# Rewriting an attention and gated feed-forward kernel around equal 512-column blocks, with loads on GpSimd's queue

## Chip, cores and metric

The kernel runs on one core of one Trainium2 chip. The metric is the device time of one execution in microseconds, lower being better. Kernels that are compared ran on the same chip in the same rounds, and only executions in the fast state are compared. Three runs of the kernel before were known, with a median of 392.63 us (390.9 to 392.78). The experiments ran on several chips, where the kernel before took 392.2 to 394.2 us (medians), so a few us between two experiments mean little.

The engines are named as the profile names them: PE is TensorE (matrix multiplications), DVE is VectorE, ACT is ScalarE, POOL is GpSimd, SP is SyncE. "Granted clock" is the share of its full clock that TensorE was allowed.

## The reference

```python
# q, k, v: (8 batches, 8 heads, 576 positions, 64), float32
def attention(q, k, v):
    theta = pi / 2 * arange(576) / 576
    phi = lambda x: concat([relu(x) * cos(theta), relu(x) * sin(theta)], -1)
    qp, kp = phi(q), phi(k)                     # 64 columns become 128
    kv = einsum('bhsf,bhsd->bhfd', kp, v)
    z = kp.sum(axis=2)
    return einsum('bhsf,bhfd->bhsd', qp, kv) / (einsum('bhsf,bhf->bhs', qp, z) + 1e-6)

x = attention(q, k, v)                          # as (4608 tokens, 512)
out = (gelu(x @ w_gate) * (x @ w_val)) @ w_out  # 512 -> 1536 -> 512
```

Each batch needs these steps: loads of q, k and v; *preps* (relu times cosine or sine, on VectorE); the *q turn*, which puts the features of the prepared q on the partitions; kv and then five numerators with their divisions; the *x turns*, which put the channels of x on the partitions; and then the three large multiplications. The large multiplications are nearly all of TensorE's work, so the rest has to be hidden behind them.

## The kernel before

All loads, the q turns and the stores go through one queue, SyncE's, in program order. The staging buffers come in threes.

```python
inp = ctx.enter_context(tc.tile_pool(name="inp", bufs=3))
xtp = ctx.enter_context(tc.tile_pool(name="xtp", bufs=3))
# ...
def load(name, src, b, half, pieces=1):
    t = inp.tile([128, 2, R * D], FP32, name=name)
    # ...
        nc.sync.dma_start(out=t[:, m:m + step], in_=view[:, 2 * half + m:2 * half + m + step])

def prep(name, b, pair, part, n=1):
    # ... for m in range(pair, pair + n):
        nc.vector.scalar_tensor_tensor(        # two sources: the input and the table
            dst[:, m, :, part * D:(part + 1) * D],
            src[:, m % 2].rearrange("p (j d) -> p j d", j=R),
            0.0,
            tab[:, :, None].to_broadcast([128, R, D]),
            op0=ALU.max, op1=ALU.mult)

def turn_q(b, pair0, n):
    # ... for i in range(2):
        nc.sync.dma_start_transpose(out=qT[b][i]..., in_=src[64 * i:64 * i + 64, ...])
```

The main loop has one 448-column block and seven of 512. In each of its twelve *slots* a block multiplies 128 columns of both weights ("gate" and "value"), and hides a piece of the next batch's attention:

```python
segs = [(576, 448)] + [(BLK * i, BLK) for i in range(2, 9)]
for si, (c0, n) in enumerate(segs, start=1):
    b = si + 1
    for jt in range(JT):
        gv_unit(c0, n, jt)
        if b < B:
            s = jt - (3 if si == 1 else 0)
            if s == 0: prep_pairs("qp", b, 0)
            if s == 1: prep_pairs("qp", b, 2)
            if s == 2: turn_q(b, 0, 4); prep_pairs("kp", b, 0)
            if s == 3: prep_pairs("kp", b, 2); cast_v(b, 0); cast_v(b, 1)
            if s == 5:
                if b + 1 < B: load_batch(b + 1)     # SyncE queue, behind the turn
                kv_unit(b)
            if 6 <= s < 6 + NT: nm_unit(b, s - 6)   # numerator and division
            if 7 <= s < 7 + NT: xt_unit(b, s - 7)   # x turned by TensorE
        if si >= 2: o_part(...)                     # output of the block before
    # ... (the first block does its last numerators after the loop)
```

## Time and profile before

| before | value |
|---|---|
| span of the profiled run | 392.7 us |
| TensorE busy | 342.5 us, 87% |
| mean granted clock | 0.950 |
| q turn, first issue to last landing | 10.5 to 12.3 us |
| loads of q, k, v, issue to landing (median) | 5.0, 7.2, 9.7 us |

These are lines of the profile's page of the kernel before: busy time by engine, three rows of the span in 40 slices (tenths), and the one queue that carries nearly everything (packets, MB, share of 16 DMA engines).

```profile
PE 342.5 (87%) x2484; PEld 177.1 (45%) x2484; DVE 204.6 (52%) x379; ACT 128.7 (33%) x242; POOL 36.8 (9%) x35
...
PE   2588955899576988998999999979997999999995
...
PEclk9999986599888998999999999989999999999999
DMA  8989908029495099309933990597056111111214
...
q1 hardware_dynamic: 57440, 55.45, 51.7%
```

TensorE is full in the later two thirds, and the losses lie early. The table by stages says where. Its columns are the stretch, its length, the busy time and instruction count of each engine, the granted clock, the DMA share and GB/s.

```profile
0.00:26.50 26.50, 13.20 (x169) 10.10 (x170) 18.10 (x30) 14.46 (x28) 11.67 (x15) 1.00 0.95 321
26.50:62.40 35.90, 29.61 (x194) 19.66 (x192) 20.32 (x46) 14.89 (x28) 11.13 (x8) 0.92 0.69 236
62.40:75.80 13.40, 7.40 (x133) 5.97 (x133) 8.31 (x21) 3.47 (x8) 0.00 (x0) 0.63 0.41 58
75.80:88.60 12.80, 12.80 (x53) 5.42 (x51) 0.00 (x0) 2.13 (x4) 0.00 (x0) 0.82 0.24 55
88.60:128.70 40.10, 29.34 (x237) 15.17 (x236) 24.22 (x43) 10.49 (x20) 4.77 (x4) 0.87 0.72 209
128.70:378.00 249.30, 239.80 (x1662) 116.27 (x1660) 133.19 (x239) 80.33 (x149) 9.21 (x8) 0.99 0.45 111
```

The start takes 26.5 us, the burst of batch 1's attention (third row) runs at a clock of 0.63, and in the last row TensorE is busy for 239.8 of 249.3 us. This is the ordering in the timeline of SyncE (start, length of the issue, what was issued):

```profile
247.79 3.47 SPq L220 DMA_TRANSPOSE qT_2743<-qp  x1
251.35 4.29 SPq L220 DMA_TRANSPOSE qT_2744<-qp  x1
255.73 2.23 SPq L359 DMA_DIRECT2D out_dram<-o_sb  x2
258.01 1.72 SPq L71 DMA_DIRECT2D qf<-in_q_dram  x2
```

The two halves of the turn are followed by a store, and only then by the loads for the batch after. The waits view has one line per turn, each of 0.8 to 2.6 us; this is the longest (engine, what waited, on what: total us, times, longest):

```profile
PE nm L260 <- DMA qT_2744<-qp: 2.6, 1, 2.6
```

### The profile page before, as it was taken

What the parts mean: (1) busy time and instruction counts of PE and PEld (TensorE: products, weight loads), DVE (VectorE), ACT (ScalarE), POOL (GpSimd) and SP (SyncE); (2) the same over time, 40 slices, a digit from 0 to 9 for tenths busy, and PEclk for the clock granted to TensorE, in tenths of its full rate; (3) what the DMA queues carried; (4) which work ended last, traced back from release to release, by engine and by line L of the source; (5) the groups of instructions that cost most, each with busy time, mean ns of one, the idle gap of its engine ahead of it and who ended that gap; (6) DMA issues with size and microseconds to landing.
All of it is one profiled execution on the core that took longest, in us unless ns stands there. A gap on an engine that the chain in (4) does not pass through costs nothing.

```text
span 392.7 us, 6081 instructions
## 1 busy us (share of the span) xinstructions
PE 342.5 (87%) x2484; PEld 177.1 (45%) x2484; DVE 204.6 (52%) x379; ACT 128.7 (33%) x242; POOL 36.8 (9%) x35
## 2 busy tenths in 40 slices
PE   2588955899576988998999999979997999999995
PEld 2365633544243444544544454535443544444442
DVE  6653496504945873587449556915693522222210
ACT  5755421213123331433333242314232333223321
POOL 1821530000202000200020011002000000000000
PEclk9999986599888998999999999989999999999999
DMA  8989908029495099309933990597056111111214
GB/s 265 381 278 362 388 15 120 2 66 357 65 222 214 2 142 321 128 1 126 340 126 44 192 350 6 86 246 258 2 84 118 29 27 42 40 27 28 52 42 95
DMA packets 57467, 55.83 MB, mean 142 GB/s; under 512 B 34912, under 2 KB 39008, under 8 KB 57440
## 3 DMA queue, kind: packets, MB, share of 16 engines
q1 hardware_dynamic: 57440, 55.45, 51.7%
q8 instruction: 19, 0.31, 0.3%
q14 instruction: 8, 0.07, 0.0%
HBM read 37.75 MB, written 9.44 MB: 120 GB/s over the span
## 4 chain that ended last, share of the span: by engine, by line
PE 71%; DMA 14%; DVE 8%; ACT 3%; POOL 2%; issue 1%; ACTq 0%; DVEq 0%; POOLq 0%
PE gv_ps L332 41%; PE o_ps L370 17%; PE gv_ps L370 6%; DVE qp L151 4%; PE xt L309 3%; PE nm L260 3%; DMA qT_1449<-qp 2%; DMA qT_3175<-qp 2%; DMA qT_2744<-qp 2%; DMA qT_1113<-qp 2%; DMA qT_702<-qp 2%; DMA qT_1881<-qp 2%; DVE hT L345 2%; DMA qT_2312<-qp 2%; DVE x_sb L273 1%; POOL pos L178 1%
## 5 line engine op out<-in xcount | busy, mean ns | idle before, releaser
L345 DVE TENSOR_TENSOR hT<-gel,gv_ps 128x512 bf16<-128x512 f32 (+2 forms) x132 | 76.0, 589 | 152.2 <-ACT gel L340 152.0
L340 ACT ACTIVATE gel<-gv_ps 128x512 f32<-128x512 f32 (+2 forms) x120 | 66.5, 555 | 203.9 <-PE gv_ps L332 203.0
L332 PE MATMUL gv_ps<-xT,wg_sb 128*128 128x512 bf16 x336 | 88.7, 388 | 0.0
L332 PE MATMUL gv_ps<-xT,wv_sb 128*128 128x512 bf16 x336 | 87.5, 383 | 0.0
L370 PE MATMUL o_ps<-wo_sb,hT 128*128 128x512 bf16 x336 | 87.1, 382 | 0.0
L332 PEld LDWEIGHTS <-wg_sb 128*128 128x128 bf16 x480 | 47.6, 101 | 64.0 <-issue 18.0
L332 PEld LDWEIGHTS <-wv_sb 128*128 128x128 bf16 x480 | 48.6, 101 | 49.9 <-issue 4.2
L370 PEld LDWEIGHTS <-hT 128*128 128x128 bf16 x432 | 41.2, 100 | 44.7 <-issue 3.5
L332 PE MATMUL gv_ps<-xT_335,wg_sb 128*128 128x288 bf16 (+1 forms) x144 | 30.0, 335 | 11.2 <-DVE hT L345 10.9
L332 PE MATMUL gv_ps<-xT_335,wv_sb 128*128 128x288 bf16 (+1 forms) x144 | 30.3, 339 | 0.0
L151 DVE SCALAR_TENSOR_TENSOR qp<-qf,cos_t 128x576 bf16<-128x576 f32 x32 | 26.0, 849 | 2.5 <-DMA qf<-in_q_dram 2.4
L151 DVE SCALAR_TENSOR_TENSOR kp<-kf,cos_t 128x576 bf16<-128x576 f32 x32 | 25.9, 851 | 1.5 <-DMA kf<-in_k_dram 1.5
L273 DVE TENSOR_TENSOR x_sb<-nm,rec 128x512 bf16<-128x512 f32 x34 | 23.5, 692 | 1.2
L370 PE MATMUL gv_ps<-wo_sb,hT 128*128 128x512 bf16 x96 | 23.3, 407 | 0.0
L151 DVE SCALAR_TENSOR_TENSOR kp<-kf,sin_t 128x576 bf16<-128x576 f32 x30 | 22.3, 788 | 0.0
L151 DVE SCALAR_TENSOR_TENSOR qp<-qf,sin_t 128x576 bf16<-128x576 f32 x30 | 21.4, 752 | 0.0
L309 PE MATMUL xt<-ident,x_sb 128*128 128x128 bf16 x144 | 15.6, 238 | 4.2 <-DVE x_sb L273 3.2
L187 POOL CAST vx_132<-vf 128x1152 bf16<-128x1152 f32 x7 | 8.7, 1250 | 112.1 <-DMA vf<-in_v_dram 77.9
L379 ACT COPY o_sb<-o_ps 128x512 f32<-128x512 f32 x28 | 16.4, 586 | 7.4 <-PE o_ps L370 7.4
L187 POOL CAST vx_134<-vf 128x1152 bf16<-128x1152 f32 x8 | 9.2, 1150 | 102.0 <-DMA vf<-in_v_dram 102.0
L317 ACT COPY xT<-xt 128x512 bf16<-128x512 bf16 (+1 forms) x34 | 16.7, 501 | 4.8 <-PE xt L309 4.7
L237 PEld LDWEIGHTS <-kp 64*128 64x128 bf16 x576 | 11.0, 100 | 9.7 <-issue 4.0
(77 smaller groups left out, 171.9 us busy)
## 6 DMA issues: line engine op xcount, KB each, us to landing
out_dram<-o_sb SPq DMA_DIRECT2D x72, 128.0 KB, 2.4
qf<-in_q_dram SPq DMA_DIRECT2D x14, 576.0 KB, 5.0
kf<-in_k_dram SPq DMA_DIRECT2D x14, 576.0 KB, 7.2
vf<-in_v_dram SPq DMA_DIRECT2D x14, 576.0 KB, 9.7
wgf<-in_moe_w_gate_dram SPq DMA_DIRECT2D x4, 768.0 KB, 6.6
wvf<-in_moe_w_val_dram SPq DMA_DIRECT2D x4, 768.0 KB, 7.8
wof<-in_moe_w_out_dram SPq DMA_DIRECT2D x4, 768.0 KB, 12.6
qf<-in_q_dram SPq DMA_DIRECT2D x4, 288.0 KB, 4.1
```

The lines of the kernel that those rows point to most:

```text
L151: nc.vector.scalar_tensor_tensor(dst[:, m, :, part * D:(part + 1) * D], src[:, m % 2].rearrange("p (j d) -> p j d", j=R), 0.0, tab[:, :, N ...
L187: copy(vx_tiles[b % 2][:, 2 * half:2 * half + 2, :, 0:D], staged["vf", b, half].rearrange("p m (j d) -> p m j d", j=R),)
L237: nc.tensor.matmul(ps[:, i, pair * (D + 1):(pair + 1) * (D + 1)], lhsT=kp[rr, pair, j, :], rhs=vx[rr, pair, j, :], start=(j == 0), stop=(j ...
L260: nc.tensor.matmul(ps[:, h // 4, (h % 4) * (D + 1):(h % 4 + 1) * (D + 1)], lhsT=qT[b][h % 2][:, h // 2, c0:c0 + 128], rhs=kv_sb[b][:, h // ...
L273: nc.vector.tensor_tensor(x, nm[:, :, :, 0:D], rec[:, :, :, None].to_broadcast([128, 2, 4, D]), op=ALU.mult,)
L309: nc.tensor.transpose(out=ps[:, ct, :], in_=x[:, ct * 128:(ct + 1) * 128], identity=ident)
L317: nc.scalar.copy(xt[:, :, base + c:base + c + m], ps[:, :, o:o + m])
L332: nc.tensor.matmul(ps[:, 0:n], lhsT=w[:, ct, js], rhs=xt[:, ct, cc:cc + n], start=(ct == 0), stop=(ct == CT - 1),)
L340: nc.scalar.activation(gel[:, 0:n], g_ps[:, 0:n], AF.Gelu)
L345: nc.vector.tensor_mul(hT[hb][:, jt, c:c + m], gel[:, o:o + m], v_ps[:, o:o + m])
L370: nc.tensor.matmul(o_ps[i], lhsT=hT[blk][:, jt, tt * 128:(tt + 1) * 128], rhs=wo_sb[:, jt, :], start=(jt == 0), stop=(jt == JT - 1),)
L379: nc.scalar.copy(o_sb, o_ps.pop(i))
```

## The change

The change is a rewrite that tries to keep TensorE full from earlier on. All blocks have 512 columns. Weights are converted by the DMA that loads them, so no engine casts them. The loads of weights and of batches 1 to 7 form one queue in a fixed order, issued by GpSimd. Preps use an instruction with one source and a scalar per partition. The eight accumulator banks are assigned by hand. Attention runs one block ahead. In batches 2 to 7, x is turned by DMA instead of TensorE.

```diff
-    wst = ctx.enter_context(tc.tile_pool(name="wst", bufs=4))
-    inp = ctx.enter_context(tc.tile_pool(name="inp", bufs=3))
+    inp = ctx.enter_context(tc.tile_pool(name="inp", bufs=2))      # now a whole batch each
+    xsp = ctx.enter_context(tc.tile_pool(name="xsp", bufs=3))
@@ weights, cut @@
-            nc.sync.dma_start(out=t[:, :, 0:n * 128], in_=src[:, :, sl])
+        nc.gpsimd.dma_start(out=wg_sb[:, :, sl], in_=wg_r[:, :, sl])
+        nc.gpsimd.dma_start(out=wv_sb[:, :, sl], in_=wv_r[:, :, sl])
@@ prep, cut @@
-            nc.vector.scalar_tensor_tensor(
+                nc.vector.tensor_scalar(
+                    o, i, 0.0, tab[:, j:j + 1], op0=ALU.max, op1=ALU.mult
+                )
@@ x, cut @@
+            nc.sync.dma_start_transpose(
+                out=xT_block(blk)[:, :, c:c + m], in_=x[o:o + m, :]
+            )
@@ the main loop, cut @@
+    for n in range(1, NB):
+        b = n + 1
         for jt in range(JT):
+            gv_unit(n, jt)
             if b < B:
+                if jt < 2:
+                    prep("q", b, jt, range(R))
+                if jt == 2:
+                    turn_q(b)
+                if jt in (2, 3):
+                    prep("k", b, jt - 2, range(R))
+                if jt == 4:
+                    kv_unit(b)
                     if b + 1 < B:
-                        load_batch(b + 1)
+                        for name in ("q", "k", "v"):
+                            for m in (0, 2):
+                                load(nc.gpsimd, name, b + 1, m, m + 2)
+                        for m in (0, 2):
+                            cast_v(b + 1, m, m + 2, pool_copy)
+                if 5 <= jt < 5 + NT:
+                    nm_unit(b, jt - 5)
+                    turn_x(b, jt - 5)
+            o_part(4 * (n - 1) + jt // 3, range(4 * (jt % 3), 4 * (jt % 3) + 4), 4 + (jt // 3) % 2, act_copy)
```

The place of the load in the program text (slot 4) says little. GpSimd has its own instruction stream and reaches the load long before TensorE reaches slot 4. What holds the load is its buffer. With two buffers, q of batch b+1 needs the buffer of batch b-1, and the program orders it behind the reads that must be finished. So what GpSimd loads beside the turn of batch b is batch b+2.

## The prediction

> **What bounds the kernel now.** TensorE. In the last stage the PE timeline repeats every 2.59 us (8 gate/value matmuls 1.73, 4 output matmuls 0.86): 0.216 us per 512-column matmul. The feed-forward's 1296 are 280 us of 392.6; 112.6 us are start, attention, waits and tail. Table of stages: first gate/value matmul at 26.5 us; block 0 until 62.4; q turn and attention burst until 75.8, clock 0.61; output projection until 88.6; the 448-column block until 128.7; seven blocks in 249.3 us (217.7 of feed-forward, 31.6 for five batches, 6.3 each); tail 14.7.
>
> Of a batch's 6.3 us PE work is 4.0 (kv 1.35, five numerators 1.4, five transposes 1.15). The chain of waits names the rest: preps, two pairs of 1.43 us between hT multiplies, stretch four slots from 2.59 to about 3.27; the q turn, 10.5 to 12.3 us from first issue to last landing, holds the first numerator 1 to 3 us.
>
> **What changes.**
> 1. Start: no staging casts; two token tiles suffice for the first half-width matmuls. Estimate from today's durations: v lands near 10 us, first gate/value matmul near 18.
> 2. Block 0: about 25 us of PE work and 3 of waits; its projection (10.4) hides batch 1's attention (4). Block 1 starts near 62 (now 88.6, though 64 columns, 2.6 us, further on).
> 3. Preps become one-source. The Trainium skill, "VectorE: DVE Perf Modes", section on the perf-mode tier table, gives fp32 SBUF single-source ops twice the rate. A traced prep takes 0.67 us back to back for 576 elements (1 per cycle plus 0.07). Estimate at double rate: 0.20 us per 256 elements, 1.8 us a slot instead of 2.7; with hT it fits 2.59.
> 4. x transposes leave PE in batches 2 to 7 (1.15 us each), but as many bytes as the q turn's join the DMA transposes.
> 5. Apparently unintended: output tiles 0 to 3 are computed after block 0 and again inside block 1: 48 matmuls, 10.4 us for nothing.
>
> **On the critical path.** 62 + 8 × 31.1 + 6 × 2.85 (kv, numerators) + 14.7 = 342.5 us, plus each batch's wait for its q turn. Preps end about 7 us into a block, so it lands near 18; the first numerator is due at 16: 2 us of wait. Traffic makes it worse: loads two batches ahead wait only for preps to free their buffers, so q's load is released just as the turn is issued, k and v soon after. "DMA: Bandwidth & Descriptors" (same skill), section "Issuing engines are not separate DMA queues", says they share 16 engines; before, one in-order queue put the turn first, and the turn alone shows a DMA share near 1.0 for 9 us; the loads take 9.6. Full sharing would cost up to 8 us per batch in blocks 1 to 4. I take 3 us for each of six batches, 18 us.
>
> **Prediction: 361 us**, 343 to 386 eight times in ten. Faster by over 2%: 0.87; within 2%: 0.09; slower: 0.04.
>
> **Right or wrong in the profile.** First gate/value matmul 16 to 21 us; block 1 begins 59 to 66; preps near 0.2 us; slots of 2.6 us at a block's start; each batch's first numerator the largest PE wait, on a DMA into qT, worse in blocks 1 to 4 than in 5 and 6; otherwise clock near 1.00; 480 output matmuls instead of 432.
>
> **What would make it wrong.** The q turn drowned by loads (then about 385, clock dropping after each wait), or winning the sharing (about 352). Preps at single rate (+1 us per slot). GpSimd's descriptors slow, so weights late and block 0 starved. x turns late for the next block.

## The result and the profile after

The rewrite gives correct outputs and takes 481.38 us (four runs, 478.76 to 482.74) where the kernel before took 391.79 us (four runs, 390.9 to 392.78). The ratio is 1.2258, 95% interval 1.2202 to 1.2313: 23% slower. Ratios here are the mean time of one kernel's fast runs over that of the other's of the same rounds, so they differ a little from the ratio of the quoted medians.

The page of the profile after:

```profile
PE 349.2 (73%) x2343; PEld 172.1 (36%) x2378; DVE 198.8 (42%) x550; ACT 105.1 (22%) x197; POOL 58.4 (12%) x82
...
PE   7599629920799405996039970599799799999996
...
PEclk9699869975699955999559995599999999999999
DMA  7999996699343995329972299642732822111113
...
q1 hardware_dynamic: 55616, 25.18, 38.2%
q0 software_dynamic: 14112, 30.15, 25.5%
```

TensorE's busy time has hardly moved (342.5 to 349.2 us), but the span is 84 us longer. There are four deep holes in the TensorE row, evenly spaced; the granted clock falls to half in each, and the DMA row is full beside them. The line of the chain of work that ended last names them, as shares of the 477.0 us:

```profile
DMA qT<-qp 30%; PE ps L310 28%; PE ps L336 16%; DVE qp L158 7%; DVE kp L158 5%; PE ps L243 3%; DVE hT L319 3%; DMA kf<-in_k_dram 1%; DVE x_sb L256 1%; PE ps L224 0%; PE ps L291 0%; PE ps L187 0%; PE ps L201 0%; DVE vx L163 0%; DVE rec L255 
```

The waits view gives the same in time lost by TensorE:

```profile
PE ps L243 <- DMA qT<-qp: 104.0, 12, 20.9
```

TensorE stood 104.0 us waiting for turned q, up to 20.9 us at once. Before, each turn had cost it 0.8 to 2.6 us.

To see when the holes arise I took the start of each block (its first write of the hidden tile by VectorE, less the 2.0 us that the first slot takes before it) and compared the lengths with the prediction's own terms. For blocks 1 to 6 that is 31.1 + 2.85 + 3 = 36.95 us.

| | block 1 starts | 1 | 2 | 3 | 4 | 5 | 6 | 7 | block 8 and tail |
|---|---|---|---|---|---|---|---|---|---|
| predicted | 62 | 36.95 | 36.95 | 36.95 | 36.95 | 36.95 | 36.95 | 31.1 | 45.8 |
| measured | 80.3 | 62.6 | 61.6 | 61.5 | 58.2 | 37.6 | 37.9 | 31.1 | 46.3 |

The sums for blocks 5 to 8 are right within a microsecond, for 5 and 6 partly by luck: the 3 us were meant for loads beside the turn, of which there are none, and block 5 spends instead 2.2 us waiting for the turn and about 1.5 in four slots that the preps hold at 2.97 us (see the end). Blocks 1 to 4 are too short by 96.0 us in the prediction and the start by 18.3; together these are all but 2 us of the 116 by which the profiled span (477.0) exceeds 361. What blocks 1 to 4 have and 5 and 6 don't is a load of a further batch: in block 5 batch 7, the last, has already been loaded.

The timelines of SyncE and of GpSimd in block 1 show what stands beside what. SyncE:

```profile
88.37 22.29 SPq L180 DMA_TRANSPOSE qT<-qp  x2
110.75 1.29 SPq L330 DMA_DIRECT2D out_dram<-o_sb  x2
```

GpSimd, with its idle time before each instruction and what ended it in brackets:

```profile
88.60 1.42 POOL L80 DMA_DIRECT2D qf<-in_q_dram  x2 [10.91 <-DVE qp L158]
94.71 1.42 POOL L80 DMA_DIRECT2D kf<-in_k_dram  x2 [4.68 <-DVE kp L158]
96.12 1.41 POOL L80 DMA_DIRECT2D vf<-in_v_dram  x2
```

The last q prep of batch 2 frees q's buffer and at the same time allows the turn. So the load of batch 4's q follows the turn's issue by 0.2 us, in this block and in the next two (151.20 after 150.96, 212.80 after 212.56). k and v follow six microseconds later, when the k preps end. The turn then lands at 122.5, 34.1 us after its issue; in blocks 2 to 4 it takes 33.3, 33.2 and 30.0 us. In blocks 5 and 6, with nothing beside, it takes 11.8 and 12.1. The loads suffer too: their medians are 12.8, 19.0 and 20.8 us instead of 5.0, 7.2 and 9.7.

The stretch in detail, in the table by windows (columns as above):

```profile
core 0: us, PE busy (x) PEld busy (x) DVE busy (x) ACT busy (x) POOL busy (x), PEclk, DMA share, GB/s
...
90.00:94.00 4.00, 3.71 (x26) 1.62 (x24) 4.00 (x15) 0.60 (x1) 0.02 (x1) 1.00 1.12 142
...
102.00:106.00 4.00, 0.00 (x0) 0.00 (x0) 0.00 (x0) 0.00 (x0) 0.00 (x0) 0.50 1.03 238
...
110.00:114.00 4.00, 0.00 (x0) 0.00 (x0) 0.00 (x0) 0.00 (x0) 0.00 (x0) 0.50 1.22 55
...
122.00:126.00 4.00, 3.43 (x15) 1.51 (x16) 1.06 (x3) 0.59 (x1) 1.15 (x1) 0.50 0.25 74
```

From 102 to 114 no compute engine works at all, the DMA engines count as fully busy, and yet from 110 to 114 they move 55 GB/s. A share near 1 tells here that packets were in flight, not that bytes flowed. The DMA view of three windows of 2 us shows it by queue (packets, MB, share of the 16 engines' time). In order they are 90 to 92 us (the turn has the engines, the load isn't yet moving), 104 to 106 us (both), and 112 to 114 us (both, in the last third):

```profile
q1 hardware_dynamic: 1046, 0.27, 102.1%
...
q0 software_dynamic: 122, 0.51, 74.2%
q1 hardware_dynamic: 165, 0.04, 41.6%
...
q1 hardware_dynamic: 135, 0.03, 90.2%
q0 software_dynamic: 15, 0.06, 21.7%
```

q1 is SyncE's queue and carries the turn, in packets of 256 bytes; q0 is GpSimd's. The turn alone gets 1046 packets through in 2 us; beside the loads it gets 165, and later 135. The time of one turn packet, as share × 32 us / packets, goes from 31 ns to 81 and then to 214 ns. The turn doesn't merely get a smaller share of a constant flow: in the last window both queues together move less than the turn alone would.

### The profile page after: what moved, and what is told of

It reads as the page before. It is cut to its first block, busy times and chain, and to the rows that moved or that the text cites. A ratio compares the mean times of both kernels' runs of the same rounds, so it can differ in the third digit from the quotient of the medians.

```text
span 477.0 us, 6176 instructions
## 1 busy us (share of the span) xinstructions
PE 349.2 (73%) x2343; PEld 172.1 (36%) x2378; DVE 198.8 (42%) x550; ACT 105.1 (22%) x197; POOL 58.4 (12%) x82
## 3 DMA queue, kind: packets, MB, share of 16 engines
q0 software_dynamic: 14112, 30.15, 25.5%
## 4 chain that ended last, share of the span: by engine, by line
PE 49%; DMA 31%; DVE 17%; issue 2%; SPq 0%; ACT 0%; DVEq 0%; ACTq 0%
DMA qT<-qp 30%; PE ps L310 28%; PE ps L336 16%; DVE qp L158 7%; DVE kp L158 5%; PE ps L243 3%; DVE hT L319 3%; DMA kf<-in_k_dram 1%; DVE x_sb L256 1%; PE ps L224 0%; PE ps L291 0%; PE ps L187 0%; PE ps L201 0%; DVE vx L163 0%; DVE rec L255 0%
## 5 line engine op out<-in xcount | busy, mean ns | idle before, releaser
L319 DVE TENSOR_TENSOR hT<-gel,ps 128x512 bf16<-128x512 f32 (+1 forms) x114 | 74.9, 657 | 140.7 <-PE ps L310 140.6
L336 PE MATMUL ps<-wo_sb,hT 128*128 128x512 bf16 x457 | 123.1, 393 | 2.1 <-issue 1.2
L310 PE MATMUL ps<-xT,wg_sb 128*128 128x512 bf16 (+1 forms) x452 | 115.8, 379 | 1.2 <-DVE xT L295 1.1
L310 PE MATMUL ps<-xT,wv_sb 128*128 128x512 bf16 (+1 forms) x448 | 115.0, 377 | 0.5
L318 ACT ACTIVATE gel<-ps 128x512 f32<-128x512 f32 (+1 forms) x114 | 65.5, 575 | 158.1 <-PE ps L310 150.5
L243 PE MATMUL ps<-kv_sb,qT 128*128 128x65 bf16 x320 | 19.6, 203 | 104.7 <-DMA qT<-qp 104.0
L336 PEld LDWEIGHTS <-hT 128*128 128x128 bf16 x480 | 45.1, 100 | 48.9 <-issue 3.8
L243 PEld LDWEIGHTS <-qT 128*128 128x128 bf16 x320 | 16.6, 104 | 116.4 <-DMA qT<-qp 107.8
L345 ACT COPY o_sb<-ps 128x512 f32<-128x512 f32 x38 | 22.3, 586 | 152.0 <-PE ps L336 150.0
L256 DVE TENSOR_TENSOR x_sb<-ps,rec 128x512 bf16<-128x512 f32 x40 | 27.7, 691 | 1.6 <-DVE rec L255 0.2
L80 POOL DMA_DIRECT2D qf<-in_q_dram x15 | 10.8, 720 | 96.0 <-DVE qp L158 93.8
L158 DVE TENSOR_SCALAR kp<-kf,cos_t 128x256 bf16<-128x256 f32 (+1 forms) x81 | 21.5, 338 | 1.4 <-DMA kf<-in_k_dram 1.4
L158 DVE TENSOR_SCALAR qp<-qf,cos_t 128x256 bf16<-128x256 f32 x72 | 19.9, 349 | 2.5 <-DMA qf<-in_q_dram 2.5
L158 DVE TENSOR_SCALAR qp<-qf,sin_t 128x256 bf16<-128x256 f32 x72 | 20.0, 349 | 0.0
L224 PEld LDWEIGHTS <-kp 64*128 64x128 bf16 x504 | 12.2, 99 | 14.6 <-DVE kp L158 9.2
## 6 DMA issues: line engine op xcount, KB each, us to landing
qf<-in_q_dram POOLq DMA_DIRECT2D x14, 576.0 KB, 12.8
vf<-in_v_dram POOLq DMA_DIRECT2D x14, 576.0 KB, 20.8
```

The costliest lines, as they stand in the source:

```text
L80: eng.dma_start(out=staged[name, b][:, m0:m1, j0 * D:j1 * D], in_=rows(srcs[name], b)[:, m0:m1, j0 * D:j1 * D],)
L158: nc.vector.tensor_scalar(o, i, 0.0, tab[:, j:j + 1], op0=ALU.max, op1=ALU.mult)
L224: nc.tensor.matmul(bank(6 + i)[:, m * (D + 1):(m + 1) * (D + 1)], lhsT=kp[rr, m, j, :], rhs=vx[rr, m, j, :], start=(j == 0), stop=(j == R ...
L243: nc.tensor.matmul(bank(b0 + h // 4)[:, (h % 4) * (D + 1):(h % 4 + 1) * (D + 1)], lhsT=qT[b][h % 2][:, h // 2, c0:c0 + 128], rhs=kv_sb[b][ ...
L256: nc.vector.tensor_tensor(x, nm[:, :, :, 0:D], rec[:, :, :, None].to_broadcast([128, 2, 4, D]), op=ALU.mult,)
L310: nc.tensor.matmul(bank(b0 + g)[:, 0:w], lhsT=wt[:, ct, js], rhs=xt[:, ct, c0:c0 + w], start=(ct == 0), stop=(ct == CT - 1),)
```

## The experiments

Thirteen kernels ran, all correct. Each is an edit of the rewrite. The letters in the expectations name the theories that they compare; each expectation spells them out. The main ones are: that the loads run beside the turn (A), that the excess over plain sharing belongs to GpSimd's software queue (B, later A2), and that the x turns by DMA are to blame (C). Times are medians, and ratios are to the kernel before in the same rounds, with 95% intervals. In e1, e2, e3, e5, e6 and e9 the place of the load in the program, or the gate before it, also lets it run only one batch ahead: beside (or after) the turn of batch b comes batch b+1, of the same size, where the rewrite has b+2.

### e1_gate: hold the loads until the turn has landed

GpSimd reads one column of both halves of the turned q before it issues the next loads. Queue and sizes stay.

```diff
+    def gate_on_turn(b):
+        for i in range(2):
+            nc.gpsimd.tensor_copy(gate, qT[b][i][:, 0, 0:1])
@@
                     if b + 1 < B:
+                        gate_on_turn(b)
                         for name in ("q", "k", "v"):
```

> Changed kernel, but GpSimd reads one column of both halves of the turned q before it issues the next batch's loads, so loads still go through GpSimd's queue but never run beside the q turn. Theory A (loads running beside the turn stretch both): the q turn takes 11 us again in every block instead of 34, the wait at the first numerator falls from 20-24 to 2-3 us in all blocks, time near 395 us (481 less 4 times about 21). Theory B (GpSimd's queue is itself slow, descriptors late): loads stay slow, 20 us and more to land, time above 440. Theory C (the turns of x make too much DMA work): no large change, above 450.

It took 390.69 us (0.9946, 0.9841 to 1.0051). All turns of blocks 1 to 5 took 11.8 to 12.4 us, and the wait for turned q fell from 104.0 to 16.6 us:

```profile
PE ps L243 <- DMA qT<-qp: 16.6, 7, 2.8
```

So the loads beside the turn are the cause of the stretch. The queue by itself isn't slow (theory B): after the turn its loads landed in 5.1, 9.3 and 12.6 us (medians). A part of the gain was lost elsewhere: the loads now fall on the x turns. The group of the division says so (busy, mean ns, idle before it, what ended that):

```profile
L256 DVE TENSOR_TENSOR x_sb<-ps,rec 128x512 bf16<-128x512 f32 x40 | 27.7, 691 | 30.9 <-DMA xT<-x_sb 29.6 <-DVE rec L255 0.2
```

VectorE waited 29.6 us for x turns to give a buffer back.

### e2_sp_queue: the loads in SyncE's queue, behind the turn

```diff
-                                load(nc.gpsimd, name, b + 1, m, m + 2)
+                                load(nc.sync, name, b + 1, m, m + 2)
```

> Changed kernel, but the loads of batches 2 to 7 are issued by SyncE in the same queue as the turns, behind the q turn in program order, as the kernel before had it. Theory A (overlap): q turn 11 us, time near 390 to 400; turns of x come behind the loads and may be late. Theory B (GpSimd's queue slow): also near 390 to 400, so this run alone doesn't separate A from B. Theory C (x turns too much): above 450.

It took 385.33 us (0.981, 0.961 to 1.001), which is not clear of noise against the kernel before. Turns took about 12 us, TensorE waited 16.7 us for them, and blocks 1 to 5 had 39.2 to 39.7 us each.

```profile
PE ps L243 <- DMA qT<-qp: 16.7, 7, 2.6
```

Block 1 began at 73.2 instead of 80.3, because batch 1's turn had been stretched too, from 12 to 19 us, by loads of batches 2 and 3 (GpSimd issued the former until 47.8 us and the latter from 62.96, and the turn ran from 49.8 to 69.3). This one word takes away 87 of the 104 us of waiting, and the profiled span shrinks by 90.6 us (477.0 to 386.4). What is left over, some 3 us, leaves room for the slower clock after each hole (0.50 from 122 to 126 us); that wasn't separated.

### e3_act_queue and e5_act_timed: the loads beside the turn, in ScalarE's queue

e3 issues the loads from ScalarE's stream just after the turn; e5 does so too, but with q released by the last q prep and k and v later, as in the rewrite.

```diff
@@ e3 @@
                     turn_q(b)
+                    if b + 1 < B:
+                        for name in ("q", "k", "v"):
+                            for m in (0, 2):
+                                load(nc.scalar, name, b + 1, m, m + 2)
@@ e5 @@
+    def on_prep(b):
+        nc.scalar.copy(agate, phi["q", b][:, NP - 1, R - 1, F - 1:F])
@@
                     turn_q(b)
+                    if b + 1 < B:
+                        on_prep(b)
+                        for m in (0, 2):
+                            load(nc.scalar, "q", b + 1, m, m + 2)
@@
-                        for name in ("q", "k", "v"):
+                        for name in ("k", "v"):
                             for m in (0, 2):
-                                load(nc.gpsimd, name, b + 1, m, m + 2)
+                                load(nc.scalar, name, b + 1, m, m + 2)
```

> Changed kernel, but the loads of batches 2 to 7 are issued by ScalarE's hardware queue, at the same place as the q turn, so that they run beside it in another queue, with no software descriptors. Theory A (overlap with any other queue): the turn stays stretched, 25 to 34 us, time 460 to 485. Theory B (only GpSimd's software queue does it): the turn takes about 20 us at most (11 of turn plus 10 of loads shared), time near 420 or below.

e3 took 413.31 us (1.0522, 1.0345 to 1.0699). The turns took 15 to 16 us and the loads landed in 4.6, 7.0 and 9.4 us (medians), as before. Theory A as I had put it, with 25 to 34 us from whatever queue, missed. But in e3 q was released 1.7 to 2.2 us before the turn, so the overlap wasn't the same, and e5 was made to mend that.

> As e3 (loads of batches 2 to 7 in ScalarE's hardware queue) but released at the moments at which the change released them: q's when q's preps end, with the turn, k's and v's after k's preps, so only the kind of queue differs from the change. Theory A2 (the excess over plain sharing belongs to GpSimd's software queue): the turn takes 15 to 21 us in blocks 1 to 4 and the time is 405 to 425 us. Theory A1 (any two queues, if the loads don't get a head start): the turn takes 28 to 34 us and the time is 460 to 485.

e5 took 410.35 us (1.0433, 1.0349 to 1.0517). The turns took 14.7, 15.0, 14.4, 18.0 and 14.8 us in blocks 1 to 5. So the same bytes, released by the same event beside the same turn, cost it about 3 us from ScalarE's queue (6 in block 4) and 18 to 22 from GpSimd's. Over this pair that is shown for the queue with all that goes with it: its packets (below), and when it starts to move. The DMA view of e5 from 92 to 94 us, while both are moving (q10 is ScalarE's queue):

```profile
q1 hardware_dynamic: 738, 0.19, 59.2%
q10 hardware_dynamic: 183, 0.39, 56.5%
```

Here four turn packets go through for each load packet, in the rewrite 1.4. Load packets have 2,304 bytes in this queue and 4,608 in GpSimd's, though the two transfers are written alike.

Two more windows of e5, 88 to 90 us and 96 to 98 us, show what that comparison leaves out:

```profile
q10 hardware_dynamic: 164, 0.38, 85.4%
...
q1 hardware_dynamic: 1786, 0.46, 101.0%
```

From 88 to 90 only the load moves, and none of the turn, although both were released together; in the rewrite the turn moves first. No run tests whether that order matters. And from 96 to 98 the turn passes 1786 packets in 2 us, where the turn alone passed 1046 at the same share of 1. So the lone turn, for all its share of 1, hadn't used up the engines, which may be why loads from ScalarE's queue cost it so little. The low cost to the turn doesn't bring the kernel near 361 us: in e5 TensorE waited 36.9 us for turned q in all, and blocks 1 to 5 took 41.9 to 45.1 us.

### e4_x_on_pe: x of batches 2 to 7 turned by TensorE again

```diff
+                if 6 <= jt < 6 + NT:
+                    turn_x_pe(b, jt - 6, 4 + (jt // 3 + 1) % 2, act_copy)
                 if 5 <= jt < 5 + NT:
                     nm_unit(b, jt - 5)
-                    turn_x(b, jt - 5)
```

> Changed kernel, but x of batches 2 to 7 is turned by TensorE and copied by ScalarE as before; loads as in the change. Theories A and B: the q turn is as stretched as before (about 34 us in blocks 1 to 4), time within 8 us of 481. Theory C (the DMA turns of x are the excess): time falls by 30 us or more.

It took 490.78 us (1.2494, 1.2356 to 1.2632), a little more than the 8 us above 481 that was expected, and the waits view has nearly the same line as the rewrite:

```profile
PE ps L243 <- DMA qT<-qp: 106.9, 12, 21.7
```

Without x turns by DMA in the loop the q turns are as long as before. Theory C falls, and x on TensorE costs about 9 us.

### e6_q_beside and e9_qk_beside: fewer loads beside the turn

Both keep GpSimd's queue and let only a part of the loads run beside the turn. In e6 q follows the last q prep, as in the rewrite, and k and v are held until the turn has landed. In e9 k too is let go, after the k preps, and v alone is held.

```diff
@@ e6 @@
+                        gate_on_prep(b)
                         for name in ("q", "k", "v"):
+                            if name == "k":
+                                gate_on_turn(b)
@@ e9 @@
+                        gate_on_prep(b)
                         for name in ("q", "k", "v"):
+                            if name == "k":
+                                gate_on_k(b)
+                            if name == "v":
+                                gate_on_turn(b)
```

> Changed kernel, but GpSimd releases only q's load beside the turn (when q's preps end) and holds k's and v's until both halves of the turned q have landed: a third of the bytes beside the turn, in the software queue. Plain sharing (bytes add): the turn takes 11 + 3.3 = about 14 us, time near 400 to 410. Stretch in proportion to the bytes beside it (23 us of stretch for 3.5 MB): about 19 us, time near 425 to 435.

e6 took 416.34 us (1.0586, 1.0498 to 1.0673). Its q turns took 14.6 to 15.6 us, near plain sharing, but the time lies above the 400 to 410 expected of that. The x turns aren't the reason: VectorE waited 7.5 us for them, less than the 29.6 of e1. TensorE waited for turned q twice as long as in e1 (16.6 us), and its mean granted clock was 0.925 (0.964 in e1):

```profile
PE ps L243 <- DMA qT<-qp: 33.9, 8, 5.9
```

> As e6, but q's and k's loads both run beside the turn, released as in the change (after q's preps, after k's preps), and only v's is held until the turned q has landed: two thirds of the bytes beside the turn in GpSimd's queue. Plain sharing: the turn takes 11 + 6.5 = about 18 us. Stretch that grows faster than the bytes (11 us alone, 15 with q, 34 with all three): 22 to 28 us, time 440 to 465.

e9 ran twice: 471.04 us, and 480.53 us in a run counted as slow, so there is no ratio. In the profiled fast run the turns of blocks 1 to 5 took 27.1, 30.7, 31.0, 26.9 and 23.3 us. Two of these lie above the 22 to 28 us expected, and so does the time above its 440 to 465. The extra time of the turn is thus about 3 us with one load beside it, 11 to 19 with two, and 18 to 22 with three, in one profiled run each. It isn't proportional to the bytes: the second load costs the most.

### e7_pieces_of_1 and e8_pieces_of_4: other sizes of a load

I had thought that the long packets of GpSimd's queue were to blame, and that more or fewer pieces would change them.

```diff
@@ e7 (twelve loads of one head pair each) @@
-                            for m in (0, 2):
-                                load(nc.gpsimd, name, b + 1, m, m + 2)
+                            for m in range(NP):
+                                load(nc.gpsimd, name, b + 1, m, m + 1)
@@ e8 (three loads of four pairs each) @@
+                            for m in (0,):
+                                load(nc.gpsimd, name, b + 1, m, m + 4)
```

> Changed kernel, but GpSimd loads batches 2 to 7 in twelve pieces of one pair of heads instead of six of two, so that I expect its packets to be 2304 bytes instead of 4608 (the size ScalarE's queue had), at the same queue, moment and bytes. Theory P (in the stretched turn each 256-byte turn packet takes about 195 ns, the time of one 4608-byte load packet; the length of the other queue's packets sets the stretch): the turn takes 18 to 24 us in blocks 1 to 4, time 415 to 440. Theory S (GpSimd's queue as such): the turn still takes 30 us or more, time above 465.

> Changed kernel, but GpSimd loads batches 2 to 7 in three pieces of all four pairs of heads instead of six of two, so that its packets may grow to 9216 bytes. Theory P: if they do, the turn takes 50 us or more and the time is above 530; if the packets stay at 4608, nothing changes and the run says nothing. Theory S: 475 to 490 whatever the packets are.

e7 took 473.32 us (1.2045, 1.1898 to 1.2191), with turns of 28 to 29 us. e8 took 483.01 and 492.56 us, with turns of 30 to 37 us; one of its two runs counts as slow, so there is no ratio. The packets had 4,608 bytes in both. So neither tests the length of a packet, and they are inconclusive on that. They do show that the number of pieces matters little in blocks 1 to 4 (batch 1's turn took 29.4 us in e7 and 19.4 in the rewrite, which stays unexplained).

### e10_cast_loads: the loads in bf16, on GpSimd's queue

Batches 1 to 7 are converted by the DMA that loads them. This gives packets of 1,152 bytes on the receiving side.

```diff
-            staged[name, b] = inp.tile([128, NP, R * D], FP32, name=name + "f")
+            if b:
+                staged[name, b] = inp.tile([128, NP, R * D], BF16, name=name + "h")
+            else:
+                staged[name, b] = consts.tile([128, NP, R * D], FP32, name=name + "f")
```

> Changed kernel, but the loads of batches 1 to 7 write bf16 (cast by the DMA), in GpSimd's queue and released as in the change. The weights' cast loads show one packet per row, so I expect packets of one row here (1152 bytes written, about half as long as the 4608-byte ones or less). Theory P (the length of the software queue's packets sets the stretch of the turn): the turn takes 15 to 22 us in blocks 1 to 4, time 400 to 435. Theory S (the software queue as such, whatever its packets): the turn takes 27 us or more, time above 455. The preps read bf16 and may be a little faster; that is worth a few us at most. The result may differ from the reference in rounding.

It took 440.93 us (1.1192, 1.1049 to 1.1335), with turns of 25.5 to 26.2 us: between what the two theories expected, so neither is right alone. Shorter packets (or fewer bytes) help, and the software queue still costs far more than ScalarE's. The DMA view of e10 from 90 to 92 us:

```profile
q0 software_dynamic: 169, 0.18, 98.2%
q1 hardware_dynamic: 341, 0.09, 37.0%
```

The turn gets 341 packets through here; in the windows shown above it got 1046 alone, 738 beside ScalarE's loads, and 165 beside GpSimd's float32 loads.

### f1_sp_once, f2_early and f3_x_buffers: toward a better kernel

f1 is e2 without the output tiles that the rewrite computes twice.

```diff
-            o_part(4 * (n - 1) + jt // 3, range(4 * (jt % 3), 4 * (jt % 3) + 4), 4 + (jt // 3) % 2, act_copy)
+            if n > 1:
+                o_part(4 * (n - 1) + jt // 3, range(4 * (jt % 3), 4 * (jt % 3) + 4), 4 + (jt // 3) % 2, act_copy)
```

> e2 (loads behind the turn in SyncE's queue) without the second computation of output tiles 0 to 3. If those 48 matmuls lie on the critical path: 10.4 us less than e2, near 375 us. If they only filled waits: the same as e2, 385.

It took 383.46 us (0.975, 0.9671 to 0.9828), close to the second of the two cases. Block 1 became 3.2 us shorter (36.3 instead of 39.5), not 10.4. Without the filling work its first slots follow the preps (in f1's timeline VectorE writes the hidden tile every 2.97 us, where eight gate and value matmuls need 1.73), and TensorE waits 2.2 us for a k prep, 1.6 for the q turn and 2.5 for an x buffer that an x turn still holds (all in block 1).

f2 prepares q of the next batch earlier, six preps to a slot from the last two slots of the block before, and turns it one slot earlier; in batch 1 it puts eight output pieces ahead of kv.

```diff
+                if jt == 0 and b > 2:
+                    prep_some("q", b, 2)
+                if jt == 1:
                     turn_q(b)
+                if jt in (1, 2, 3):
+                    prep_some("k", b, jt - 1)
+                if jt in (10, 11) and b + 1 < B:
+                    prep_some("q", b + 1, jt - 10)
```

> f1, and q's preps from the last two slots of the block before, preps six to a slot instead of nine, the turn issued one slot earlier, and the projection of block 0 ordered so that more of it comes before batch 1's first numerator. If what is left of the wait for the turn (about 2.4 us a batch, 7 batches, more at batch 1) and of the prep slots (2.97 us instead of 2.59, four a block) is on the critical path: 20 us less than f1, 350 to 360 us. If the turns of x, behind the loads in the one queue, then come late for the next block: 365 or more.

It took 361.05 us (four runs, 359.73 to 364.43; 0.9199, 0.9122 to 0.9275). The wait for turned q fell to 4.1 us, and the x turns now stand out: VectorE waited for them to free the buffers of x.

```profile
L256 DVE TENSOR_TENSOR x_sb<-ps,rec 128x512 bf16<-128x512 f32 x40 | 27.7, 692 | 14.4 <-DMA xT<-x_sb 13.2
```

f3 is f2 with six buffers for x instead of three:

```diff
-    xsp = ctx.enter_context(tc.tile_pool(name="xsp", bufs=3))
+    xsp = ctx.enter_context(tc.tile_pool(name="xsp", bufs=6))
```

> f2 with six buffers for x instead of three. In f2 the numerators' last step waits 13 us in all for turns of x that stand behind the loads. If that wait is on the critical path: 5 to 12 us less than f2 (361), 349 to 356. If TensorE had slack there: 359 to 362.

It took 349.66 us (four runs, 348.65 to 351.21; 0.8919, 0.887 to 0.8968), 11% faster than the kernel before. Its wait on x's buffers is gone from that group, and TensorE is busy almost throughout:

```profile
PE 319.6 (92%) x2330; PEld 160.2 (46%) x2330; DVE 199.7 (58%) x550; ACT 102.9 (30%) x193; POOL 33.2 (10%) x46
```

Blocks 2 to 6 take 32.8 to 33.7 us there, against the 33.95 (31.1 + 2.85) that the prediction's terms give without any wait.

| kernel | loads of the next batch | q turn in blocks 1 to 4, us | time, us |
|---|---|---|---|
| before | SyncE queue, behind the turn | 10.5 to 12.3 | 391.79 |
| rewrite | GpSimd queue, beside | 30.0 to 34.1 | 481.38 |
| e1 | GpSimd queue, held until it landed | 11.8 to 12.4 | 390.69 |
| e2 | SyncE queue, behind | about 12 | 385.33 |
| e5 | ScalarE queue, beside, same release | 14.4 to 18.0 | 410.35 |
| e6 | GpSimd queue, q alone beside | 14.6 to 15.6 | 416.34 |
| e10 | GpSimd queue, beside, half the bytes landed | 25.5 to 26.2 | 440.93 |
| f3 | SyncE queue, behind; turn earlier; six x buffers | 10.8 to 12.4, waited for in block 1 only | 349.66 |

## Why the prediction was wrong

It said 361 us and faster; 481 was measured. Point by point:

- **The step that failed** is the last of its sum: "Full sharing would cost up to 8 us per batch in blocks 1 to 4. I take 3 us for each of six batches, 18 us." The mechanism, the place and even the moment were right: q's load was released 0.2 us after the turn's issue, the first numerator was the largest wait, on a DMA into the turned q, and it was far worse in blocks 1 to 4 than in 5 and 6. The size was wrong. Beside the loads the turn took 30.0 to 34.1 us instead of about 12, so the sharing cost it 18 to 22 us, well over the 8 called an upper bound. Where the term has 18 us for all six batches, TensorE waited 104.0 us for turned q (8.9 of them at batch 1). For blocks 1 to 4 the sum is 96.0 us short, and e1 and e2, which change only when these loads run and (e2) in which queue, take nearly all of the waiting away. The sum was too short without any overlap as well: e2 took 385.33 us, its block 1 began 11 us late and its blocks 1 to 5 took 39.2 to 39.7 us where the sum has 36.95.
- **Why the bound was no bound.** It compared two durations, each measured alone, as if the DMA engines passed as many bytes when two queues are busy as when one is. The Trainium skill, "DMA: Bandwidth & Descriptors", section "Issuing engines are not separate DMA queues", says that transfers interleave on the same 16 engines whoever issued them, and I read "interleave" as a fair division of a constant rate. Neither queue behaves so. Beside ScalarE's the turn loses less: e5 shows about 3 us extra in most blocks. That this is the number I took is luck, since no measurement stood behind it. Beside GpSimd's the turn loses more: from 112 to 114 us the two together moved 0.09 MB where the turn alone moves 0.27.
- **The stated way of going wrong was named but mis-sized too**: "The q turn drowned by loads (then about 385 ...)". The drowning happened and cost four times that allowance: 96 us in blocks 1 to 4, where 24 were allowed in all.
- **"Block 1 starts near 62" was wrong**: 80.3. Of the 18.3 us, 7.1 are the same cause at batch 1, whose turn was stretched to 19 us by the loads of batches 2 and 3 (block 1 starts at 73.2 in e2). The remaining 11 I can only describe: the sum hid batch 1's attention under the output work of block 0, but the turn is issued at 49.8 only, so even an undisturbed one of 12 us holds the first numerator until 62, where the sum had block 1 begin; and kv waited 4.4 us for v.
- **"First gate/value matmul 16 to 21 us" was right**, at the edge: 20.9 us, against 26.5 before; its own estimate was 18.
- **"Preps near 0.2 us" was wrong**, at little cost. The timeline of VectorE after shows nine preps of 256 elements in 2.45 us, between two writes of the hidden tile, and eighteen of 128 elements (the first line) in 3.62:

```profile
8.15 3.62 DVE L158 TENSOR_SCALAR kp<-kf,cos_t 128x128 bf16<-128x128 f32 x18 [1.43 <-DMA kf<-in_k_dram]
...
82.28 0.69 DVE L319 TENSOR_TENSOR hT<-gel,ps 128x512 bf16<-128x512 f32 x1 [1.13 <-PE ps L310]
82.89 2.45 DVE L158 TENSOR_SCALAR qp<-qf,cos_t 128x256 bf16<-128x256 f32 x9
85.25 0.68 DVE L319 TENSOR_TENSOR hT<-gel,ps 128x512 bf16<-128x512 f32 x1
```

  About the double rate is there. One prep lasts 0.28 us (128 elements) or 0.35 (256), so they follow one another at (3.62 - 0.28) / 17 = 0.196 and (2.45 - 0.35) / 8 = 0.263 us. Thus 128 more elements cost 0.067 us, or 1.9 per ns; the old preps did 576 in 0.67 us, 0.86 per ns with their fixed part. The fixed part was the error: 0.13 us by the same two numbers, not the 0.07 taken over from the old two-source preps. The slot therefore repeats at 2.97 us (82.28 to 85.25) instead of fitting 2.59. Before, the same stretch repeated at 3.28 us:

```profile
241.09 0.69 DVE L345 TENSOR_TENSOR hT<-gel,gv_ps 128x512 bf16<-128x512 f32 x1 [2.12 <-ACT gel L340]
...
244.37 0.68 DVE L345 TENSOR_TENSOR hT<-gel,gv_ps 128x512 bf16<-128x512 f32 x1
```

- **"480 output matmuls instead of 432" was right**, and calling that 10.4 us "for nothing" was half right. f1 took these away and block 1 gained 3.2 us, since most of this work stood where TensorE would have waited for preps and turns.
- **The x turns by DMA do no harm in the rewrite** (e4), as the prediction hoped. VectorE waits for them as soon as loads fall beside them: 29.6 us in e1, 7.5 in e6.

What is shown: the loads beside the turn cause its stretch (e1, e2); the excess over plain sharing comes with GpSimd's queue, against ScalarE's (e5 against the rewrite); the stretch isn't proportional to the number of loads (e6, e9, one profiled run each). What stays open is why. GpSimd's queue differs from ScalarE's in at least three things: its kind ("software" against "hardware" in the profile), the length of its packets (4,608 against 2,304 bytes) and the moment when its load begins to move. e7 and e8 failed to separate the first two. e10 lies between, but it also halves the bytes that land, so it doesn't separate them either. One candidate can be set aside for the crawl itself. The Trainium skill, "SBUF — State Buffer", section "SBUF: two separate sides", describes transfers issued by GpSimd that stall because VectorE holds a shared port while descriptors should be written. From 102 to 114 us VectorE ran nothing at all, and GpSimd's last issue instruction had ended at 97.5, yet both transfers crawled. It isn't set aside for the start of the load, which was issued at 88.6 and moved its first packet at 92.5, while VectorE was busy from 86 to 94 us; e1's, issued at 93.2 with neither preps nor the turn beside it, moved at 94.6. Another candidate is the sharing by whole packets that "DMA: Bandwidth & Descriptors" gives in its section "Queues, rings and completion order". The 165 turn packets of 256 bytes to 122 load packets of 4,608 from 104 to 106 us look like it (if the profile's packets are that page's), but the last window, with 135 turn packets to only 15 load packets and turn packets of 214 ns, does not. No run here shows what the engines did in that time.

## What to carry to other kernels

A transfer on the critical path is protected by the order of the queue it shares with others; when loads move to another queue, ask which event releases them and what is in flight at that moment, and hold them back if it is that transfer. Don't cost two overlapping transfers by adding their lone durations, least of all across kinds of queue: measure the overlap first, because here the same bytes beside the same turn cost about 3 us from one queue and about 21 from another. And when a repair shows the next wait (turn, then buffers of x), follow it: the one-word repair only brought the rewrite level with the kernel before (0.981, not clear of noise), and the three steps after it (f1 to f3) made it 11% faster.

## What the Trainium skill lacked or had wrong

- "DMA: Bandwidth & Descriptors", section "Issuing engines are not separate DMA queues": it says that transfers interleave, but nothing of the case where two together are slower than one after the other. Here a DMA transpose took 30.0 to 34.1 us beside three loads from GpSimd's queue, 14.4 to 18.0 beside the same loads from ScalarE's, and about 12 alone, and the GpSimd loads took 12.8 to 20.8 us instead of 5.1 to 12.6 (e1, the same queue after the turn). It adds that starting transfers from several engines saves only the time of issuing them; the rewrite against e2 shows that it can also cost (481 against 385 us), and e5 that the cost differs by queue.
- The same page doesn't compare the two kinds of queue by packet length: one and the same load shows packets of 4,608 bytes on GpSimd's queue and of 2,304 on ScalarE's. Nor does it tell that cutting it into more or fewer pieces leaves that length alone (4,608 bytes in e7 and e8).
- "SBUF — State Buffer", section "SBUF: two separate sides": it gives one reason for slow transfers from GpSimd, a VectorE instruction that holds a port. Here they crawled for 12 us with VectorE idle, so it is not the only one.
- "VectorE: DVE Perf Modes": its section "The TRN2 errata — SBUF-src ops pay a fixed extra latency per instruction" says that the fixed part of an instruction measured about 150 cycles where a formula gives 58. Here 0.13 us were found for one-source float32 preps back to back, between the two and nearer to the measured one (at the 0.96 GHz that "SBUF — State Buffer" gives for VectorE, 150 cycles are 0.156 us and 58 are 0.060, both estimates). The section "The perf-mode tier table" lacks nothing here: beside the rate it gives 1227 ns for 2,048 elements, which leaves a fixed part of about 0.16 us (an estimate). I used its rate alone, and so my prep was 0.20 instead of 0.26 us.
